# Landmark sums of two batches by adding DMA transfers, one path for the first batch's exponentials, more constants' products and a new order in a Nystrom attention and squared-ReLU kernel

## The chip, the core and the metric

The kernel runs on one core of a Trainium2 chip. The metric is the device time of one execution in microseconds (us). The profile of an execution gives the start and length of every instruction on the engines PE (TensorE's matmuls; PEld is its weight loads), DVE (VectorE), ACT (ScalarE), POOL (GpSimd) and SP (SyncE), and the DMA transfers.

## The reference: what is computed

q, k and v have 8 batches, 8 heads, 576 tokens and 64 columns. Per head, 32 landmarks are the means of 18 tokens each of q and of k. Three softmaxes follow: A (576 x 32, all queries against the key landmarks), B (32 x 32, landmarks against landmarks) and C (32 x 576, query landmarks against all keys). Z starts as B transposed over the product of two norms and goes through six steps of Z = 2 Z - Z B Z. The attention result A Z C v of all heads, 4608 tokens by 512 columns, goes through a block of two matrices.

```python
q_lm = q.reshape(B, H, m, S // m, D).mean(axis=3)     # m = 32, S // m = 18
k_lm = k.reshape(B, H, m, S // m, D).mean(axis=3)
A = sm(q, k_lm); Bm = sm(q_lm, k_lm); C = sm(q_lm, k)
for _ in range(6):
    Z = 2 * Z - Z @ Bm @ Z
x = A @ Z @ C @ v                                     # 4608 x 512 over all heads
g = np.maximum(x @ w_in, 0.0) ** 2                    # 4608 x 2048
out = g @ w_out
```

## The kernel before, in words

**One program, batch after batch.** All 8 heads of a batch lie on 128 partitions as 2 rows (r) of 4 heads (c) of 32 landmarks. POOL's queue issues all loads; most convert float32 to bf16 on the way. q and k of a batch go to X (`load_qk`, two transfers a tensor, L426), v to V (`load_v`, L442), the weights to w_in and w_out (L450, L457). There are three buffers of X and of V.

**The work of a batch** is a set of named operations, which carry the batch's number: T (transposes of q and k on DVE, L471), lm (landmark sums), lme (their scaling to bf16), lmt (their transpose), B, Bmx, Bsb, Bex, ... (softmax of B, L561 to L644), N and U (the six steps: N on PE at L713 or L718, U on DVE at L727; bd builds N's block-diagonal operand on POOL or DVE, L650), SC or SS (scores of C and A), Cmx, Cex, Cnr, CT (softmax of C), CV (C times v, L835), Zm and ZC (Z times that, L861, L869, L879, L882), W and We (times w_in, L906, and its copy out of PSUM to WP, L413, L417), SA, At, Amx, Asb, Aex, Asu, Arc, Aml, Ap, Ab (softmax of A and its transpose to AT). `ffn1` then multiplies WP with AT (F, L1079), takes the ReLU (R, L1100 on ACT or L1102 on DVE) and the square (Q, L1107 on ACT, L1109 on DVE or POOL) into G. `ffn2` multiplies G with w_out for 128 tokens at a time (O0 to O35 in four parts each, L1126), copies the sum (Oe) and stores it (St, SP's queue).

**Landmark sums.** Batches 0 to 2 add 18 tokens on PE with an identity (L502, L509). Batches 3 to 7 (`ROWS`) load q and k a second time: `load_xs` (L429) brings them as bf16 to XS, 96 partitions of 6 tokens for each head, in two transfers lx (L432), and `landmarks_rows` (L479) multiplies them with a 96 x 32 matrix of ones, 24 matmuls a batch (L487), into one bank of PSUM. One instruction then scales the sums to LM (lme, L415 on ACT or L419 on DVE).

**Softmax of A in batches 0 and 1.** It is computed with tokens on partitions, in two units u; batch 0 cuts each unit into a and b. The row maximum comes from `Amx` (L974) on DVE. Then either DVE subtracts it (Asb, L985) and ACT takes one exponential over all rows (Aex, L987), or, for the entries of `BY_ROW` (batch 0, unit 1, a and b), ACT takes the exponential row by row with the negative maximum as its bias, 10 instructions a piece (L980).

**The order is written out.** Every operation has a list of engines it may run on and costs in a small planner (`Plan`). The string `ORDER` gives the sequence of all operations, `/A`, `/D` or `/P` the engine where it isn't the first of its list, and `@` the PSUM bank. Each engine works off its share of that sequence in the planned order of starts and waits in place for whatever is late. POOL, too: a transfer that must wait for something holds up POOL's later loads and arithmetic. Software transfers use 8 slots in turn, and the ninth waits for the first to land.

**Constants' products.** Until the first O, the planner fills gaps of PE with matmuls of constants (`fillers`, `fill`, L1200), which write into a free bank and which nothing reads. A gap lies between the planned end of one operation and the planned start of the next, and products are added while the planned busy share of some stretch of 3.41 us is under a goal (0.55 before 30 us, 0.45 behind).

Of the kernel before, what the change touches and what calls it, by code (L numbers as in the profile page):

```python
# [264 lines left out]
def kernel(  # L265
# [195 lines left out]
    def attention(b):  # L461
# [477 lines left out]
        for u in range(2) if b in TOKENS else ():  # L939
# [27 lines left out]
            cuts = [0, 2 * n, 4 * n] if b in FIRST else [0, 4 * n]  # L967
            for j, (x0, x1) in enumerate(zip(cuts, cuts[1:])):
# [4 lines left out]
                op(f"Amx{b}.{u}{z}", {"DVE": v_(w)}, lambda e, s3=s3, p3_=p3_, pS=pS, at=at, neg=NM.get((b, u, z)):
                   nc.vector.tensor_reduce(s3(0)[:, at] if neg is None else neg[:, 0:at.stop - at.start],  # L974
                                           p3_(pS)[:, at], axis=AX.X, op=ALU.max, negate=neg is not None),
                   R=[pS], W=kx_("amx"))

                def rows(e, nm=NM.get((b, u, z)), sa3=sa3, p3_=p3_, pS=pS, x0=x0, x1=x1):
                    for x in range(x0, x1):
                        nc.scalar.activation(sa3[:, x], p3_(pS)[:, x], AF.Exp, bias=nm[:, x - x0:x - x0 + 1])  # L980
# [391 lines left out]
```

## Time and profile before

| what | us |
|---|---|
| median of 3 runs | 259.12 (259.1 to 259.36) |
| the profiled execution | 259.55 |
| its span in the profile | 257.8 |
| PE busy | 248.5 |
| DVE busy | 211.5 |
| ACT busy | 176.3 |
| POOL busy | 71.5 |
| loads on POOL's queue, MB | 24.25 |

The profiled execution's own time is 1.75 us above its span: that part lies around the instructions. Times of rows below are from the start of the span. A busy PE isn't PE at its peak, since the ends of matmuls are modelled. Consecutive instructions of one engine overlap by some tens of ns in the rows, so that the distance of two starts is the better measure of what one costs in a stream.

### The profile page before, as it was taken

What the parts mean: (1) busy time and instruction counts of PE and PEld (TensorE: products, weight loads), DVE (VectorE), ACT (ScalarE), POOL (GpSimd) and SP (SyncE); (2) the same over time, 40 slices, a digit from 0 to 9 for tenths busy, and PEclk for the clock granted to TensorE, in tenths of its full rate; (3) what the DMA queues carried; (4) which work ended last, traced back from release to release, by engine and by line L of the source; (5) the groups of instructions that cost most, each with busy time, mean ns of one, the idle gap of its engine ahead of it and who ended that gap; (6) DMA issues with size and microseconds to landing.
All of it is one profiled execution on the core that took longest, in us unless ns stands there. A gap on an engine that the chain in (4) does not pass through costs nothing.

```text
span 257.8 us, 7581 instructions
## 1 busy us (share of the span) xinstructions
PE 248.5 (96%) x3093; PEld 140.5 (54%) x3093; DVE 211.5 (82%) x549; ACT 176.3 (68%) x343; POOL 71.5 (28%) x122
## 2 busy tenths in 40 slices
PE   6979999999999999999999999999999999999993
PEld 2546565557554567465555466465454575466542
DVE  2779897987999999998998999888999989667221
ACT  3465779669896898888566499596663897357300
POOL 8566846643353260550210400021100100000000
PEclk9999999999999999999999999999999999999999
DMA  6999999999999999899613991025100350231044
GB/s 100 200 191 201 204 210 208 208 224 233 235 203 220 221 212 220 137 202 223 154 21 69 170 205 30 4 45 122 43 3 3 81 123 3 57 79 31 4 106 97
DMA packets 25123, 34.18 MB, mean 133 GB/s; under 512 B 2432, under 2 KB 14464, under 8 KB 25088
## 3 DMA queue, kind: packets, MB, share of 16 engines
q0 software_dynamic: 19168, 24.25, 55.6%
q1 hardware_dynamic: 5760, 9.31, 14.2%
q8 instruction: 24, 0.39, 0.6%
q10 hardware_dynamic: 160, 0.13, 0.2%
q14 instruction: 11, 0.09, 0.1%
HBM read 48.50 MB, written 9.44 MB: 225 GB/s over the span
## 4 chain that ended last, share of the span: by engine, by line
PE 84%; DVE 7%; DMA 3%; POOL 2%; issue 1%; ACT 1%; POOLq 0%
PE ps L1126 46%; PE ps L1079 23%; PE ps L906 3%; DMA X<-in_q_dram 3%; PE ps L835 2%; PE ps L487 1%; PE ps L749 1%; DVE SA L1032 1%; PE ps L713 1%; POOL X L426 1%; PE ps L1005 1%; PE ps L1200 1%; ACT SA L980 1%; PE ps L744 1%; PE ps L718 1%
## 5 line engine op out<-in xcount | busy, mean ns | idle before, releaser
L1126 PE MATMUL ps<-w_out,G 128*128 128x512 bf16 (+1 forms) x592 | 138.3, 374 | 0.0
L1126 PEld LDWEIGHTS <-G 128*128 128x128 bf16 x592 | 54.0, 98 | 54.7 <-issue 5.8
L1100 ACT ACTIVATE RS<-ps 128x576 bf16<-128x576 f32 (+2 forms) x104 | 63.7, 652 | 13.3 <-PE ps L1079 8.9
L1079 PE MATMUL ps<-AT,WP 128*128 128x288 bf16 (+2 forms) x512 | 72.0, 286 | 0.0
L1079 PEld LDWEIGHTS <-WP 128*128 128x128 bf16 x512 | 48.6, 98 | 20.6 <-issue 1.9
L1107 ACT ACTIVATE G<-RS 128x576 bf16<-128x576 bf16 (+2 forms) x54 | 35.9, 686 | 2.0 <-DVE RS L1102 1.6
L1109 DVE TENSOR_TENSOR G<-RS 128x576 bf16<-128x576 bf16 (+2 forms) x72 | 31.1, 447 | 6.8 <-ACT RS L1100 6.4
L471 DVE STREAM_TRANSPOSE TT<-X 128x576 uint32<-128x576 uint32 x32 | 24.0, 759 | 4.8 <-DMA X<-in_k_dram 4.2
L413 ACT CAST WP<-ps 128x1024 bf16<-128x1024 f32 (+1 forms) x23 | 21.8, 978 | 7.9 <-PE ps L906 7.8
L413 ACT COPY OS<-ps 128x512 f32<-128x512 f32 (+1 forms) x25 | 14.2, 571 | 18.1 <-PE ps L1126 18.0
L650 POOL TENSOR_TENSOR BD<-ST,blkb 128x256 bf16<-128x256 bf16 x15 | 10.9, 725 | 46.5 <-DVE ST L727 46.5
L790 ACT ACTIVATE C<-ps,sm 128x576 bf16<-128x576 f32 x16 | 14.4, 904 | 12.3 <-DVE sm L787 11.9
L1102 DVE TENSOR_SCALAR RS<-ps 128x576 bf16<-128x576 f32 (+2 forms) x24 | 17.9, 747 | 5.5 <-PE ps L1079 4.7
L442 POOL DMA_DIRECT2D V<-in_v_dram x24 | 12.9, 539 | 18.4 <-PE ps L835 15.1
L417 DVE COPY OS<-ps 128x512 f32<-128x512 f32 x12 | 8.3, 689 | 9.8 <-PE ps L1126 9.8
L727 DVE SCALAR_TENSOR_TENSOR ST<-ST,ps 128x128 bf16<-128x128 bf16 (+1 forms) x48 | 12.7, 264 | 2.6 <-PE ps L713 2.4
L1200 PE MATMUL ps<-onesb 128*128 128x512 bf16 (+1 forms) x38 | 11.9, 402 | 1.5 <-DVE onesb L349 1.5
L787 DVE TENSOR_REDUCE sm<-ps 128x1 f32<-128x576 f32 x16 | 11.8, 741 | 1.4 <-PE ps L718 1.2
L417 DVE CAST WP<-ps 128x1024 bf16<-128x1024 f32 (+1 forms) x11 | 12.2, 1119 | 0.3 <-PE ps L906 0.2
L1032 DVE STREAM_TRANSPOSE SA<-ps 128x320 f32<-128x320 f32 (+1 forms) x24 | 10.1, 456 | 0.3 <-PE ps L744 0.3
L906 PE MATMUL ps<-w_in,ZC 64*32 64x512 bf16 x256 | 10.2, 382 | 0.0
L426 POOL DMA_DIRECT2D X<-in_q_dram x16 | 8.9, 559 | 4.5 <-DVE sm L644 2.5
(144 smaller groups left out, 292.2 us busy)
## 6 DMA issues: line engine op xcount, KB each, us to landing
out_dram<-OS SPq DMA_DIRECT2D x70, 128.0 KB, 2.5
X<-in_k_dram POOLq DMA_DIRECT2D x16, 288.0 KB, 8.9
X<-in_q_dram POOLq DMA_DIRECT2D x16, 288.0 KB, 10.3
XS<-in_k_dram POOLq DMA_DIRECT2D x5, 576.0 KB, 9.6
XS<-in_q_dram POOLq DMA_DIRECT2D x5, 576.0 KB, 7.5
V<-in_v_dram POOLq DMA_DIRECT2D x8, 288.0 KB, 8.8
w_in<-in_moe_w_in_dram POOLq DMA_DIRECT2D x8, 256.0 KB, 10.3
w_out<-in_moe_w_out_dram POOLq DMA_DIRECT2D x4, 512.0 KB, 10.1
```

The lines of the kernel that those rows point to most:

```text
L413: nc.scalar.copy(o, i)
L417: eng(e).tensor_copy(o, i)
L471: op(f"T{b}.{t}{r}", {"DVE": v_(576) + 0.02}, lambda e, r=r: nc.vector.transpose(tt[:, t, r].rearrange("p s m e -> p (s m e)").bitcast(U32 ...
L790: op(f"Cex{b}.{r}", {"ACT": a_(576) + 0.27}, lambda e, r=r: nc.scalar.activation(Cs[r][:].rearrange("p x u -> p u x"), cbanks(r), AF.Exp, ...
L906: nc.tensor.matmul(ps[quad(pos_a(c, r)), pW.at + r, :], lhsT=zcs[r][half, pos_c(c, r), :], rhs=w_in[half, c, 512 * ch:512 * ch + 512], sta ...
L1079: nc.tensor.matmul(ps[:, ph.at + i, 0:w], lhsT=wp[:, r, 128 * ff:128 * ff + 128], rhs=at[:, r, t0:t0 + w], start=(r == 0), stop=(r == 1))
L1100: nc.scalar.activation(rs, pair(ph, w), AF.Relu)
L1102: nc.vector.tensor_scalar(out=rs, in0=pair(ph, w), scalar1=0.0, scalar2=None, op0=ALU.max)
L1107: nc.scalar.activation(g, rs, AF.Square)
L1109: eng(e).tensor_tensor(g, rs, rs, ALU.mult)
L1126: nc.tensor.matmul(bank(po)[:, 0:c1 - c0], lhsT=G[:, f, lo:lo + P], rhs=w_out[:, f, c0:c1], start=(f == 0), stop=(f == NF - 1))
L1200: nc.tensor.matmul(ps[:, j, 0:w], lhsT=onesb[:, 0:P], rhs=x[:, 0:w], start=True, stop=True)
```

## The change

**1. Adding transfers.** `ROWS` is cut to batches 3, 4, 5; batches 6 and 7 become `ADDED`. For them `load_sums` takes the place of `load_xs`: the 18 tokens of a landmark are three groups of 6, and three transfers a tensor, la6.00, la6.01, la6.02 (q) and la6.10, la6.11, la6.12 (k), bring one group each as float32 to the same place ACC. The first writes, the second and third add; each waits until the one before it has landed. ACC lies in the memory of XS (ACC of batch 6 in the half that held q, of batch 7 in the half that held k), so that the first also waits for the last reader of XS. DVE then adds 6 groups of 64 columns in two reduces a batch (lmc, 768 elements a partition) and lme scales them from SBUF. The 24 matmuls of each of the two batches are gone. The planner counts an adding transfer as 1.5 times 786432 bytes, which is what it counts for one lx.

**2. Exponentials of batch 0, unit 1.** `BY_ROW` is empty: 20 instructions of ACT go, two subtractions on DVE (Asb0.1a, Asb0.1b) and two exponentials over 320 elements on ACT come.

**3. Constants' products.** The goal before 30 us rises from 0.55 to 0.9. A gap begins where the planner's PE is free again, its wait for instructions included.

**4. The planner's fetch of PE's instructions** (256 in 6.2 us until 60 us, 3.8 until 110 us, 2.5 behind; before 6.2 until 140 us and 3.8 behind) **and a new order** of all operations, with other engines and banks: 8 more R on DVE, 6 fewer We, 4 fewer Cnr and 3 fewer Oe on DVE, 3 more Q of batch 0 on POOL among them.

```diff
-                    fetched = max(t, fetched + (self.FETCH_LOADED if t < LOADED else self.FETCH))
+                    fetched = max(t, fetched + (self.FETCH_LOADED if t < 60.0 else self.FETCH if t < 110.0 else 2.5))
...
-            a, b = o.start, o.start + o.engs["PE"]
+            a, b = o.start, o.end
...
-            if share(t) >= (0.55 if t < 30 else 0.45) or not near:
+            if share(t) >= (0.9 if t < 30 else 0.45) or not near:
...
-    XS = mk("XS", [96, 2, H, 6, D], BF16)
+    XS = mk("XS", [P, 2, H, 6, D], BF16)
+    ACC = [XS[:, i].rearrange("p h j d -> p (h j d)").bitcast(F32)
+           .rearrange("p (t r s d) -> p t r s d", t=2, r=2, d=D) for i in range(2)]
...
+    def load_sums(b):
+        for j in range(SEG // 6):
+            for t in range(2):
+                src = (q, k)[t][b].rearrange("(r c) (m s) d -> (c m) r (s d)", r=2, s=SEG)
+                op(f"la{b}.{t}{j}", {"POOL": 0.95}, lambda e, j=j, t=t, src=src: nc.gpsimd.dma_start(
+                    ACC[b % 2][:, t].rearrange("p r s d -> p r (s d)"), src[:, :, 6 * D * j:6 * D * (j + 1)],
+                    accum_op=ALU.add if j else ALU.bypass),
+                   R=[("ACC", b % 2, t)] if j else [], W=[("ACC", b % 2, t), *([] if j else [("XS", b % 2)])],
+                   nbytes=ADD_COST * 786432, queue="sw")
...
+        def landmarks_added():
+            acc, ls, kS = ACC[i2], LS[:, 0, 0:256].rearrange("p (t r d) -> p t r d", t=2, d=D), ("LS", 0)
+            for t in range(2):
+                op(f"lmc{b}.0{t}", {"DVE": v_(768)}, lambda e, t=t: nc.vector.tensor_reduce(
+                    ls[:, t], acc[:, t].rearrange("p r s d -> p r d s"), axis=AX.X, op=ALU.add),
+                   R=[("ACC", i2, t)], W=[(kS, t), (kS, "w")])
+            op(f"lme{b}.0", {"ACT": a_(256), "DVE": v_(256, True)}, lambda e: copy(e, lm[:], ls, scale=LMS),
+               R=[(kS, 0), (kS, 1)], W=[("LM", i2, r) for r in range(2)], port=("DVE",))
...
-ROWS = (3, 4, 5, 6, 7)
+ROWS = (3, 4, 5)
+ADDED = (6, 7)
+ADD_COST = 1.5
...
-BY_ROW = ((0, 1, "a"), (0, 1, "b"))
+BY_ROW = ()
...
```

The new order up to the first F's of batch 0 (from the maximum of B to F0.2), and the order before in the same stretch:

```
after:
Bcs0 Btr0 Cex0.0 Amx0.0b BBT0@7 Bnm0 SA0.1@1 Brn0 Yi0 Zi0/P Amx0.0a Asb0.0b win00 N0.0@4 Crc0 CT0.0 lm1.0@5
Aex0.0b win01 U0.0 Asb0.0a N0.1@6 Amx0.1a Aex0.0a lm1.0a win20 U0.1 Asb0.1a N0.2@7 Asu0.0a
Aex0.1a lm1.0b U0.2 T1.01 win21 N0.3@0 lme1.0 CV0@6,3 Cmk0 U0.3 Amx0.1b N0.4@5 Asu0.0b CVe0.0/A
lmt1.0 CVe0.1/A U0.4 bk1/P Arc0.0a Asb0.1b N0.5@5 B1@6 Arc0.0b CR0@4 Aex0.1b U0.5 Bmx1 Aml0.0b/P
CRe0/A Bsb1 Zd0@5 Asu0.1b Bex1 SA1.0@1 Zm0 Aml0.0a/P Bsu1 Asu0.1a ZC0@2 ldv2.11 Arc0.1b Amx1.0
Ap0.0@4 ZCe0 wout0 SA1.1@6 Arc0.1a Brc1 Ab0.0/A Aml0.1a Asb1.0 Bml1/P Aml0.1b/P Bmb1/A Aex1.0
W0.1@2 Amx1.1 W0.3@4 We0.1 Blo1/P ldv1.11 Ap0.1@0 Asb1.1 wout1 We0.3 F0.6@2 Ab0.1 ldk2.1 W0.0@6
R0.6 F0.4@4 wout2 We0.01/D We0.00 Bcs1@0 F0.20@2 R0.4 ldq2.1 Bnm1 Bad1 F0.2@6
before:
Bcs0 Btr0 Cex0.0 Amx0.1a BBT0@5
Bnm0 SA0.0@7 Brn0 Aex0.1a c8 Yi0 Zi0/P Amx0.1b win21 Amx0.0b N0.0@0 lm1.0@4 U0.0 Amx0.0a Asb0.0b
N0.1@1 Aex0.1b lm1.0a U0.1 win20 Asb0.0a CT0.0 N0.2@6 lm1.0b U0.2 T1.01 win31 N0.3@5 lme1.0 win30
U0.3 CV0@6,0 Aex0.0a Asu0.1a lmt1.0 Asu0.0a bk1/P CVe0.0/A B1@2 Asu0.1b N0.4@4 c10 Aex0.0b U0.4
Bmx1 Arc0.1a Bsb1 N0.5@5 Asu0.0b Aml0.1a/P Bex1 SA1.1@6 c14/A Bsu1 Arc0.1b Brc1 CVe0.1/A Crc0
U0.5 wout0 Cmk0 Aml0.1b CR0@2 Amx1.1 Zd0@4 Bml1/P CRe0/A Bmb1/A Zm0 Ap0.1@2 Blo1 Arc0.0a Arc0.0b
Asb1.1 Aml0.0a/P Bcs1@0 Ab0.1/A SA1.0@5 Btr1 Aml0.0b/P Aex1.1 Bnm1 Bad1 BBT1@3 Brn1 ldv1.11 ZC0@4
Yi1 Ap0.0@7 Zi1 ZCe0 Amx1.0 wout1 N1.0@6 Ab0.0/A W0.1@2 U1.0 W0.0@0 ldk2.1 Asb1.0 We0.1 N1.1@4
wout2 W0.2@6 U1.1 We0.01/D We0.00 ldk2.0 N1.2@5 F0.4@2
```

And three stretches of the new order around the adding transfers of batch 6:

```
la6.00 Q2.0 N3.4@1 F2.11@4 Aex3.0 R2.4/D O9.0@2 la7.00 lme5.0 U3.4 R2.11 bd3.5/D F2.8@6 Q2.4
...
F2.12@0 Q2.14/A Arc3.1 Arc3.0 ZC3@3 Aml3.0 O10.1
R2.12 la6.10 R2.15 ZCe3.0/D O10.2 Btr4 Ab3.0 ZCe3.1 Q2.15/A lmt5.0 la6.01 T4.01 W3.0@5 Q2.12/A
W3.3@3 W3.2@0 bt4/D ldq6.0 We3.0 O9.2 Aml3.1 ldq5.1 Bct4 Ab3.1 O9.3 We3.2 la7.10 T5.11 F3.2@5
We3.3 T4.00 O10.3 Bnm4 R3.2 Bad4 Brn4 BBT4@3 T5.10 F3.0@0 Zi4/P Oe9.0 ldk6.1 F3.1@4 Yi4 R3.0 St9
...
bd4.3/D R3.3 la6.02 Brc5 T4.10 O12.3 R3.5 Bml5/P F3.4@4 ldq7.1 Btf5 Oe12.0 Bcs5 F3.6@0 Q3.3
...
Q3.15/A bd5.2/D CV4@3,5 Asu4.1 N5.2@2 O14.3 Arc4.1 CVe4.1/A CVe4.0 T6.11 la6.12 ZC4@5 O13.3
Oe14.0 U5.2 ZCe4.0/D ldv6.10 bd5.3/D St14 ZCe4.1/D O15.3 Aml4.1 Oe13.0 ldk7.0 N5.3@2 ldv7.11
W4.0@3 Oe15.0 U5.3 W4.2@5 Ab4.1 ldq7.0 W4.3@0 We4.0 St15 Aml4.0 O16.0@2 la7.12 We4.2 O16.1 Ab4.0
St13 lmc6.00 bd5.4 We4.3 F4.0@3 W4.1@6 R4.0/D O16.2 We4.1 O16.3 lmc6.01 N5.4@3 SS5.0@0,4,6
lme6.0/D Oe16.0 U5.4 lmt6.0
```

More of the change, by code (lines that the diff above doesn't have):

```diff
@@ L1173, in loads @@
             load_xs(b)
+        elif what == "sums":
+            load_sums(b)
         elif what == "win":
@@ L1245 @@
-N0.1@1 Aex0.1b lm1.0a U0.1 win20 Asb0.0a CT0.0 N0.2@6 lm1.0b U0.2 T1.01 win31 N0.3@5 lme1.0 win30
-U0.3 CV0@6,0 Aex0.0a Asu0.1a lmt1.0 Asu0.0a bk1/P CVe0.0/A B1@2 Asu0.1b N0.4@4 c10 Aex0.0b U0.4
-Bmx1 Arc0.1a Bsb1 N0.5@5 Asu0.0b Aml0.1a/P Bex1 SA1.1@6 c14/A Bsu1 Arc0.1b Brc1 CVe0.1/A Crc0
-U0.5 wout0 Cmk0 Aml0.1b CR0@2 Amx1.1 Zd0@4 Bml1/P CRe0/A Bmb1/A Zm0 Ap0.1@2 Blo1 Arc0.0a Arc0.0b
-Asb1.1 Aml0.0a/P Bcs1@0 Ab0.1/A SA1.0@5 Btr1 Aml0.0b/P Aex1.1 Bnm1 Bad1 BBT1@3 Brn1 ldv1.11 ZC0@4
-Yi1 Ap0.0@7 Zi1 ZCe0 Amx1.0 wout1 N1.0@6 Ab0.0/A W0.1@2 U1.0 W0.0@0 ldk2.1 Asb1.0 We0.1 N1.1@4
```

210 lines of the change are left out of this document (106 added, 104 removed).

## The prediction

> **What bounds the kernel now.** I read the page first: the busy shares, the slices of PE and its clock, and the shares of the chain that ended last.
>
> ```profile
> PE 248.5 (96%) x3093; PEld 140.5 (54%) x3093; DVE 211.5 (82%) x549; ACT 176.3 (68%) x343; POOL 71.5 (28%) x122
> ...
> PE   6979999999999999999999999999999999999993
> ...
> PEclk9999999999999999999999999999999999999999
> ...
> PE 84%; DVE 7%; DMA 3%; POOL 2%; issue 1%; ACT 1%; POOLq 0%
> ```
>
> PE is busy from the second slice on at full granted clock, and the chain is PE for 84%. A gain must take work off PE or bring PE's own work forward. The table of windows says where that is possible.
>
> ```profile
> 18.00:24.00 6.00, 4.99 (x156) 3.46 (x158) 5.90 (x24) 4.11 (x19) 3.66 (x6) 1.00 1.19 185
> 24.00:30.00 6.00, 5.61 (x92) 3.19 (x92) 5.44 (x21) 3.35 (x8) 4.88 (x10) 1.00 1.24 206
> 36.00:42.00 6.00, 6.00 (x76) 3.78 (x75) 4.16 (x8) 4.40 (x8) 3.16 (x6) 1.00 1.17 210
> 102.00:108.00 6.00, 6.00 (x139) 2.87 (x128) 5.97 (x20) 4.20 (x9) 2.40 (x4) 1.00 0.79 127
> 132.00:138.00 6.00, 6.00 (x121) 2.81 (x120) 5.93 (x13) 3.25 (x8) 1.11 (x2) 1.00 0.53 85
> 252.00:258.00 6.00, 1.77 (x17) 1.35 (x14) 0.69 (x1) 0.37 (x1) 0.00 (x0) 0.94 0.38 83
> ```
>
> Columns: window, length, then busy time of PE, PEld, DVE, ACT and POOL, then clock, DMA share, GB/s. Before 30 us PE's business is partly constants, and DVE (5.90 of 6) is the engine that works without pause. From 36 us PE is full. The last window's PE ends about 4 us before the span does; that tail (copy, store, landing) keeps its form in the new order: the last four parts of O35, one copy, two stores.
>
> ```profile
> L1200 PE MATMUL ps<-onesb 128*128 128x512 bf16 (+1 forms) x38 | 11.9, 402 | 1.5 <-DVE onesb L349 1.5
> ```
>
> So the 30.5 us before the first F hold about 12 us of PE time that computes nothing. That start, the landmarks on PE, and a few waits in the middle are all that can be won.
>
> **Part 1, landmark sums: what goes.** The first and the last of five pieces of the chain show what a batch's 24 matmuls cost.
>
> ```profile
> 61.20 0.77 PE ps L487 x24
> ...
> 159.86 0.77 PE ps L487 x24
> ```
>
> Each is 0.77 us long, with PE's work directly before and behind. Batches 6 and 7 lose 2 x 0.77 = 1.5 us, at a place where PE is full: **-1.5 us**.
>
> **Part 1: what comes.** DVE gets two reduces of 768 elements a batch. The nearest rows:
>
> ```profile
> L1043 DVE TENSOR_REDUCE smA<-SA 128x20 f32<-128x640 f32 x6 | 4.8, 796 | 0.3 <-ACT SA L1041 0.3
> L1043 DVE TENSOR_REDUCE smA<-SA 128x16 f32<-128x512 f32 x6 | 4.0, 659 | 0.0
> ```
>
> From 512 to 640 elements a reduce grows by 137 ns, so 768 take some 0.93 us. Two a batch and two batches are 3.7 us of DVE; lme stays about what it was. DVE is nearly full there (5.93 and 5.97 of 6 us), but the new list also takes 6 We of 1.1 us and 3 Oe of 0.7 us off it and gives it 8 R of 0.75 us: its total hardly moves. PE need not wait as long as DVE's order holds, so I cost the reduces at 0; without that cover they cost up to 3.7 us.
>
> The transfers are the unknown. Nothing in this trace adds on the way. Nearest rows:
>
> ```profile
> XS<-in_k_dram POOLq DMA_DIRECT2D x5, 576.0 KB, 9.6
> XS<-in_q_dram POOLq DMA_DIRECT2D x5, 576.0 KB, 7.5
> ...
> DMA to landing us min/median/max: 6.4/9.3/14.7
> ```
>
> The third row is that of the line which issues XS. One adding transfer reads a third of the float32 bytes of an XS transfer and writes 384 KB instead of 576. If bytes alone count, it lands no later than XS does, 6.4 us; if reading back what is there costs as much again as an XS transfer, twice the median, 19 us. I take the median, 9.3 us: it lies in the stretch where the DMA share falls from 0.79 to 0.53, but three follow each other. Now the room. PE's work between two names of the new list is counted with rows of the chain: four O matmuls 0.86, F of batch 3 on 0.49, CV 0.76, a W (8 matmuls) 0.28.
>
> ```profile
> 102.25 0.76 PE ps L835 x72
> ...
> 110.33 0.56 PE ps L906 x16
> ...
> 118.05 0.49 PE ps L1079 x4
> 118.60 0.86 PE ps L1126 x4
> ```
>
> From la6.00 to la6.01 stand 5 O, 6 F, 1 CV: 8.0 us. From la6.01 to la6.02 6 O, 6 F, 4 W: 9.2 us. From la6.12 to the reduce that needs it (lmc6.01) 6 O, 1 F, 4 W: 6.8 us. At 9.3 us POOL waits 1.3 and 0.1 us at the two, which the next POOL work in the list (Zi4, some 4 us of PE later; Bml5, one O later) absorbs; DVE could wait 2.5 us at lmc6.01, but DMA has little queued there (0.53), so I go to the lower end for that one: below 6.8 us, no wait. Cost taken: **0**; bounds 0 and the price of the second rival.
>
> By the Trainium skill, "DMA: Bandwidth & Descriptors", section "Rules for kernel authors", an accumulating DMA reads its destination and writes it later with nothing holding the bytes in between, so each must wait for the semaphore of the one before; its section "Anatomy of one DMA" fits 2.0 us plus bytes over 436e3. By that fit 384 KB would land in an estimated 2.9 us, and no wait would be left; the row's 6.4 us as the minimum is longer.
>
> **Part 2, the exponentials, and the new order up to the first F.** The timeline of the stretch that sets the start:
>
> ```profile
> 14.76 0.66 POOL L450 DMA_DIRECT2D w_in<-in_moe_w_in_dram  x1
> ...
> 15.67 1.87 ACT L980 ACTIVATE SA<-ps,NM1a 128x32 f32<-128x32 f32 x10
> 16.01 0.23 DVE L674 TENSOR_TENSOR ST<-ps,sm 128x64 bf16<-128x64 f32 x1
> 17.57 0.49 DVE L974 TENSOR_REDUCE NM1b<-ps 128x10 f32<-128x320 f32 x1 [1.33 <-ACT SA L980]
> 17.98 0.41 DVE L974 TENSOR_REDUCE smA<-ps 128x8 f32<-128x256 f32 x1
> 18.31 0.28 DVE L727 SCALAR_TENSOR_TENSOR ST<-ST,ps 128x128 bf16<-128x128 bf16 x1
> 18.50 0.42 DVE L974 TENSOR_REDUCE smA<-ps 128x8 f32<-128x256 f32 x1
> ...
> 24.02 0.20 DVE L727 SCALAR_TENSOR_TENSOR ST<-ST,ps 128x64 bf16<-128x64 bf16 x1
> ```
>
> DVE sat idle 1.33 us until the row by row exponentials were done, and U0.0 (18.31) stood behind it. With one reader of that PSUM piece that wait goes, and two subtractions of 320 elements come. In a stream the starts lie 0.33 us apart for 256 elements (17.98, 18.31), 0.41 for 320 (17.57, 17.98), 0.19 for a U (18.31, 18.50). In the new list DVE has between Yi0 (16.01) and U0.5: five pieces of 256 (1.7), three of 320 (1.2), five U (0.95), CT 0.39, T 0.67, lmt 0.23, Cmk0 and three reciprocals (0.45): 5.6 us. With 0.2 for Yi0 and a little waiting U0.5 starts at 22.1 instead of 24.02, **1.9 us earlier**. Then Bmx1, Bsb1, one sum (0.7 us) and Zm0 at 23.0.
>
> ```profile
> 25.49 0.41 DVE L861 TENSOR_TENSOR ZM<-ps,CRS 128x256 bf16<-128x256 f32 x1
> 26.69 0.63 PE L955 MATMUL ps<-BK,TT 128*128 128x128 bf16 x8
> 27.16 0.70 PE L1200 MATMUL ps<-onesb 128*128 128x512 bf16 x3
> 27.79 0.22 PE L664 MATMUL ps<-Bt 32*32 32x32 bf16 x8
> 27.94 0.30 PE L879 MATMUL ps<-ZM,CV 128*64 128x32 bf16 x8
> 28.93 0.63 PE L906 MATMUL ps<-w_in,ZC 64*32 64x512 bf16 x16
> 29.41 2.42 ACT L413 CAST WP<-ps 128x1024 bf16<-128x1024 f32 x3
> 30.49 1.53 PE L1079 MATMUL ps<-AT,WP 128*128 128x256 bf16 x12
> ```
>
> ZM was ready at 25.9, yet ZC (27.94) stood on PE behind batch 1's scores and BBT1. The new list moves BBT1 and Bcs1 behind the first F. ZC0 then runs at 23.5, Ap0.0 and SA1.1 behind it (0.5 and 0.8), W0.1 at 25.2. What comes last is ACT's queue: Aex1.0 stands before We0.1 and needs Asb1.0, which DVE reaches 2.6 us after Zm0 (Asu0.1a 0.41, Amx1.0 and Asb1.0 0.6 each, Aml0.1a 0.5, small ones 0.5), at 25.9; Aex1.0 0.65, We0.1 1.0: F0.6 at **27.7 instead of 30.49, 2.8 us earlier**. The loads allow it, just: the pieces that W0.1 needs are now the second and fourth of w_in, the fourth is issued at 14.76, and the median to landing gives 25.1.
>
> ```profile
> w_in<-in_moe_w_in_dram POOLq DMA_DIRECT2D x8, 256.0 KB, 10.3
> ```
>
> Not all of that is kept. N1.0 to N1.2, Bcs1 and BBT1 (five rows of 0.2) and one more W (0.28) now run behind the first F: 1.2 us. And F0.2 waits for two copies to WP that start when W0.0 is done, about 0.4 us. Net **-1.2 us**. Bounds: 0 if DVE loses what the missing wait gave, -2.8 if the moved products fall into gaps.
>
> **Part 3, constants.** They fill gaps only; a product too many delays the next PE work by its length, 0.22 us for 512 columns at worst, and only where PE's next operand is ready earlier than planned. Cost taken 0, bounds 0 and +1 us. The granted clock is full without more of them, so nothing is gained either.
>
> **Part 4, the rest of the order.** One wait in the middle can go:
>
> ```profile
> 65.50 0.27 PE L744 MATMUL ps<-TT,LT 32*32 32x256 bf16 x1 [0.56 <-ACT RS L1100]
> ```
>
> The second half of batch 2's scores waited for ACT to free a bank. In the new list an O and more work stand between that F and SS2.0, and more again before SS2.1: -0.5 us. Loads come earlier for batches 3 and 4; the tightest, lx4.1 to lm4.0, keeps 10 O and 7 F, 12 us, against 9.6 us to landing. Unknown here: -1 to +4 us, since every engine waits in place.
>
> **Sum.** -1.5 - 1.2 - 0.5 = -3.2 us from the profiled execution's 259.55: 256.35. Its span is 257.8, 1.75 us lie around it and stay. The median shown is 0.43 us below the profiled run, so the time to compare is **255.9 us**.
>
> **Rivals.**
> - *The start gains nothing.* DVE is full from 18 to 30 us, and two subtractions join it. If Zm0 comes as late as before, only the landmarks and the bank wait remain, less the moved products: -1.5 - 0.5 + 1 = -1.0, **258.1 us**. Against it: 1.33 us of idle DVE and 2 us of ready ZM. Chance 0.20.
> - *The adding transfers become the wait (slower).* If each lands in 19 us, POOL stands 11 us at la6.01 and 10 us at la6.02, with X, V, Zi4 and Bml5 behind, and DVE, in order, 12 us at lmc6.01 with all R, Q and U behind it. PE can run on for perhaps 2 us. It decides from about 10 us at la6.12 (6.8 of room, 3.2 of gain to eat). At 14 us PE loses some 7 - 2 at lmc6.01 and 2 in POOL's part: +7, **263 us**. For it: three in a row were never run here; against it: a DMA share of 0.5. Chance 0.14.
> - *The new order waits elsewhere.* A late bank or operand in the middle, as the 0.56 us above but larger; 3 to 6 us eat the gain: **259 to 262 us**. Chance 0.16.
> - *More than said.* The moved products vanish in gaps and more bank waits go: -5, **254 us**. Chance 0.07.
>
> **How the numbers follow.** The forecast (254.5 to 257.5) has 0.43. Faster by over 0.2% (below 258.6), which is about what a measurement of this kernel can tell from no change: forecast 0.43, more 0.07, three quarters of the first rival, 0.15, together 0.65. Within 0.2%: 0.05 of it and 0.04 of the waiting order: 0.09. Slower: 0.14 and 0.12: 0.26. The range leaves out the upper part of the slow cases and the lower part of the best one: 253.9 to 261.5.
>
> **What would show it.** Right: L487 with 72 matmuls instead of 120; no L980; DVE without idle between 16 and 18 us; L879 near 23.5 and the first L1079 near 27.7 us; landings of the adding transfers under 9 us and no wait of DVE for them; PE full from 36 us. Wrong: POOL idle for a landing of its own adding transfer beyond 2 us, DVE waiting at the reduces, the first L1079 after 29.5, or windows after 36 us in which PE falls below 5.9.

## The result, and the profile after

| kernel | median, us | ratio to the kernel before, same chip | span of the profiled execution, us |
|---|---|---|---|
| before | 259.22 (259.1 to 259.36) | 1 | 257.8 |
| changed | 262.1 (261.81 to 263.53) | 1.0122 [1.0085, 1.0159] | 260.1 |

The change makes the kernel 1.2% slower, some 3.1 us, where 3.2 us faster were forecast: outside the range, and on the other side. From the page of the changed kernel, the busy shares, and the shares of the chain that ended last:

```profile
PE 249.1 (96%) x3051; PEld 139.4 (54%) x3051; DVE 217.0 (83%) x552; ACT 179.4 (69%) x326; POOL 82.7 (32%) x132
...
PE 72%; DVE 16%; DMA 4%; POOL 3%; issue 2%; ACT 2%; SPq 0%; DVEq 0%; POOLq 0%; ACTq 0%
```

PE has as much to do as before, but the chain is PE for 72% and no longer for 84%; DVE's part went from 7% to 16%. The windows of the changed kernel (columns as in the prediction) say where PE lacks work:

```profile
24.00:30.00 6.00, 5.05 (x73) 3.15 (x71) 5.56 (x14) 3.92 (x8) 5.76 (x10) 1.00 1.23 205
36.00:42.00 6.00, 5.28 (x40) 2.96 (x38) 6.00 (x7) 5.31 (x10) 3.25 (x4) 1.00 1.16 212
42.00:48.00 6.00, 4.98 (x72) 2.04 (x71) 5.25 (x15) 2.25 (x5) 5.48 (x7) 1.00 1.17 209
48.00:54.00 6.00, 5.67 (x159) 3.63 (x159) 4.42 (x18) 1.81 (x4) 3.38 (x5) 1.00 1.20 206
144.00:150.00 6.00, 5.44 (x87) 2.60 (x88) 5.97 (x14) 3.60 (x6) 1.81 (x2) 1.00 0.72 178
168.00:174.00 6.00, 5.55 (x49) 2.68 (x47) 5.86 (x14) 4.05 (x7) 1.76 (x3) 1.00 0.61 98
```

The kernel before had PE at 6.00 in each of the last five. So two places behind the first F lose: 36 to 54 us (2.1 us), and 144 to 174 us (1.0 us in these two windows). (The window 24.00:30.00, in front of it, comes back with few_constants below.) In the first place, DVE's 36.00:42.00 holds only 7 instructions in 6.00 busy us. The timeline of DVE there, then that of POOL:

```profile
36.12 0.77 DVE L483 STREAM_TRANSPOSE TT<-X 128x576 uint32<-128x576 uint32 x1
36.81 2.57 DVE L694 TENSOR_TENSOR ST<-Bf,sm 128x64 bf16<-128x64 f32 x1
39.30 0.76 DVE L483 STREAM_TRANSPOSE TT<-X 128x576 uint32<-128x576 uint32 x1
...
42.09 0.66 DVE L1015 TENSOR_REDUCE smA<-SA 128x16 f32<-128x512 f32 x1
42.68 0.86 DVE L377 TENSOR_TENSOR blk<-blkb 128x64 bf16<-128x64 bf16 x1
43.47 0.21 DVE L697 TENSOR_TENSOR ST<-ps,sm 128x64 bf16<-128x64 f32 x1
```

```profile
36.46 1.26 POOL L1135 TENSOR_TENSOR G<-RS 128x640 bf16<-128x640 bf16 x1
...
38.24 1.05 POOL L1135 TENSOR_TENSOR G<-RS 128x512 bf16<-128x512 bf16 x1
42.24 1.25 POOL L1135 TENSOR_TENSOR G<-RS 128x640 bf16<-128x640 bf16 x1 [2.96 <-DVE RS L1128]
```

L694 is Zi1, L377 is c8 (64 columns each), L1135 on POOL is a square Q of batch 0; the new order gives POOL five of them instead of two. Zi1 takes 2.57 us and ends with the second of two squares; c8 takes 0.86 us and ends with the third. Both read two tiles of SBUF. The transpose at 36.12 and the sum at 42.09, which run beside the same squares, read one tile of SBUF each and take what they take elsewhere (0.77 and 0.66 us). Who pays is seen in the waits of PE in the changed kernel (total us, times, longest):

```profile
PE ps L772 <- DVE RS L1128: 0.9, 1, 0.9
PE ps L741 <- DVE ST L697: 0.8, 1, 0.8
...
PE ps L736 <- DVE BD L673: 0.4, 1, 0.4
PE ps L858 <- issue: 0.3, 1, 0.3
```

The first two are the scores SC1.0 and the first step N1.0, at 42.2 and 43.7 us: late banks and late operands of a DVE that is 3 us behind. The third falls at 172.8 us and belongs to the second place, where the reduces of the landmark sums stand:

```profile
L509 DVE TENSOR_REDUCE LS<-XS x4: 1437/1460/1484, 142.9 to 169.8; 128x128 f32<-128x768 f32 x4
```

Minimum, median and maximum in ns: 1460, not the estimated 930. The adding transfers themselves were no trouble. Their line in the changed kernel shows the issues, who waited for them, and the landing:

```profile
L442 POOL DMA_DIRECT2D XS<-in_q_dram x6: 742/1228/1705, 99.9 to 147.6; - x6
L442 POOL DMA_DIRECT2D XS<-in_k_dram x6: 709/1261/1284, 105.6 to 138.9; - x6
...
  POOL XS L442: 0.7, 1
...
DMA to landing us min/median/max: 4.7/6.4/9.7
```

POOL waited 0.7 us, once, for its own earlier piece, and DVE never. (Before the first of them POOL also waited 4.6 us for the last reader of XS on PE.)

### The profile page after: what moved, and what is told of

Its sections match the earlier page's. It is cut to its first block, busy times and chain, and to the rows that moved or that the text cites. A ratio compares the mean times of both kernels' runs of the same rounds, so it can differ in the third digit from the quotient of the medians.

```text
span 260.1 us, 7502 instructions
## 1 busy us (share of the span) xinstructions
PE 249.1 (96%) x3051; PEld 139.4 (54%) x3051; DVE 217.0 (83%) x552; ACT 179.4 (69%) x326; POOL 82.7 (32%) x132
## 4 chain that ended last, share of the span: by engine, by line
PE 72%; DVE 16%; DMA 4%; POOL 3%; issue 2%; ACT 2%; SPq 0%; DVEq 0%; POOLq 0%; ACTq 0%
PE ps L1152 38%; PE ps L1105 21%; PE ps L929 3%; DMA X<-in_q_dram 3%; PE ps L858 2%; DVE sm L810 2%; DVE TT L483 1%; PE ps L772 1%; PE ps L1230 1%; DVE LS L509 1%; DMA out_dram<-OS 1%; PE ps L499 1%; POOL X L428 1%; PE ps L736 1%; DVE ZM L892 1%
## 5 line engine op out<-in xcount | busy, mean ns | idle before, releaser
L1126 ACT ACTIVATE RS<-ps 128x576 bf16<-128x576 f32 (+2 forms) x96 | 58.7, 652 | 14.6 <-PE ps L1105 10.5
L1133 ACT ACTIVATE G<-RS 128x576 bf16<-128x576 bf16 (+2 forms) x59 | 38.9, 682 | 3.1 <-DVE RS L1128 2.5
L415 ACT COPY OS<-ps 128x512 f32<-128x512 f32 (+1 forms) x28 | 16.2, 579 | 22.3 <-PE ps L1152 17.2
L1135 DVE TENSOR_TENSOR G<-RS 128x576 bf16<-128x576 bf16 (+2 forms) x64 | 27.9, 449 | 2.1 <-ACT RS L1126 1.3
L415 ACT CAST WP<-ps 128x1024 bf16<-128x1024 f32 (+1 forms) x29 | 26.8, 978 | 4.0 <-PE ps L929 3.7
L1128 DVE TENSOR_SCALAR RS<-ps 128x576 bf16<-128x576 f32 (+2 forms) x32 | 24.0, 752 | 3.6 <-PE ps L1105 1.7
L673 POOL TENSOR_TENSOR BD<-ST,blkb 128x256 bf16<-128x256 bf16 x12 | 8.4, 701 | 45.9 <-DVE ST L750 44.5
L419 DVE COPY OS<-ps 128x512 f32<-128x512 f32 (+1 forms) x9 | 5.7, 645 | 10.0 <-PE ps L1152 10.0
L736 PEld LDWEIGHTS <-BD 128*128 128x128 bf16 x72 | 6.4, 98 | 7.8 <-POOL BD L673 1.4
L428 POOL DMA_DIRECT2D X<-in_k_dram x16 | 9.7, 608 | 2.0 <-DVE BD L673 1.1
```

Source lines behind the costliest of these rows:

```text
L415: nc.scalar.copy(o, i)
L1126: nc.scalar.activation(rs, pair(ph, w), AF.Relu)
L1128: nc.vector.tensor_scalar(out=rs, in0=pair(ph, w), scalar1=0.0, scalar2=None, op0=ALU.max)
L1133: nc.scalar.activation(g, rs, AF.Square)
L1135: eng(e).tensor_tensor(g, rs, rs, ALU.mult)
```

## The experiments

The theory (A): what was lost is DVE standing still beside POOL's squares at 36 to 44 us, and reduces that are half as long again as thought on a DVE that has no room for them. Rivals: DVE simply has too much to do in the new order's start (B); the loss is all elsewhere (C), in the new order behind 47 us (D), or in the constants' products. All runs, each beside the kernel before on the same chip:

| run | edit | median, us | ratio | span, us |
|---|---|---|---|---|
| zi_apart | Zi1 on POOL, c8 early | 260.34 | 1.0022 [1.0007, 1.0038] | 258.7 |
| sq_on_dve | the five squares on DVE | 260.75 | 1.0042 [1.0023, 1.0061] | 258.8 |
| rows_67 | landmarks of 6, 7 on PE again | 262.05 | 1.0082 [1.0064, 1.01] | 260.1 |
| sum_straight | reduces without stride | 260.9 | 1.0052 [1.0029, 1.0075] | 259.0 |
| changed_again | none | 262.7 | 1.0109 [1.0068, 1.015] | 262.1 |
| fill_old | constants as before | 263.0 | 1.0132 [1.0091, 1.0174] | 260.9 |
| start_only | new order to 47 us, then the old | 260.24 | 1.002 [1.0, 1.0041] | 258.1 |
| zi_and_adds | zi_apart, adds for reduces | 259.07 | 0.9967 [0.9947, 0.9986] | 256.5 |
| added_alone | old order, adding transfers, adds | 262.09 | 1.01 [1.008, 1.0121] | 259.9 |
| zi_and_adds_again | as zi_and_adds | 258.99 | 0.9976 [0.9963, 0.9989] | 257.2 |
| few_constants | zi_and_adds, no constants after 8 us | 258.33 | 0.995 [0.9932, 0.9968] | 256.4 |
| fewer_late | zi_and_adds, none after 17 us | 259.78 | 1.001 [0.9995, 1.0025] | 257.6 |

**changed_again** gives the base. 

> The changed kernel once more, as the base beside which the runs on this chip are read: 1.012 of the kernel before, 262 us, with Zi1 near 2.6 us long on DVE and the gaps before SC1.0 and N1.0 near 1 us each. If the 1.012 came from few runs and not from the change, it comes out below 1.008.

It is 1.0109: the loss is the change's, about 1.1 to 1.2%. But the spans of the two profiled executions are 260.1 and 262.1 us, and the second shows why the times of this kernel scatter more than those of the kernel before. Windows of 1 us of changed_again:

```profile
25.00:26.00 1.00, 0.05 (x3) 0.04 (x4) 0.99 (x4) 0.00 (x0) 0.88 (x2) 0.99 1.25 205
26.00:27.00 1.00, 0.67 (x11) 0.66 (x12) 0.68 (x2) 0.27 (x1) 0.92 (x2) 0.50 1.24 210
...
28.00:29.00 1.00, 1.00 (x23) 0.34 (x20) 0.36 (x1) 0.68 (x3) 0.77 (x2) 0.50 1.22 206
```

PE does nearly nothing for a microsecond in front of ZC0 (0.05 of 1.00; ZC0 comes at 25.95), and then the granted clock is 0.50 for some 3 us, just where W and F come: the first F is at 30.19, not at 28.46. In the first profile the same stretch had a clock of 1.00. This isn't rare. Each execution's mean granted clock is on record: of the ten of the changed kernel (four of the first measurement, six of this one) four have 0.990 to 0.993 and take 263.3 to 263.9 us, and six have 0.997 to 1.000 and take 261.4 to 262.2 us. So a part of the loss in the medians is this, some 1.5 us in the executions that have it, and differences by ratios and by spans are both given below; the spans are compared with that of the first profile, whose clock was full at this place.

**zi_apart.** Only two small instructions move; the squares stay on POOL.

```diff
-Zi1 ... c8 SC1.0@4,6
+c8 SC0.1@4 ... Zi1/P ... SC1.0@4,6
```

> The changed kernel (262.1 us) with two small DVE instructions of batch 1's start taken away from POOL's squares of batch 0: Zi1 (2.57 us in the changed kernel's row, 0.21 usual) runs on POOL behind those squares, and c8 (0.86 us there, 0.17 usual) stands on DVE ahead of SC0.1. The five squares stay on POOL. Theory A (a DVE instruction that reads two tiles of SBUF stands still while POOL squares; PE loses 1.10 us before SC1.0 and 0.97 us before N1.0 by it): the two gaps shrink to under 0.5 us together, 260.1 to 260.7 us. Theory B (DVE simply has too much to do between 30 and 44 us in this order, the long row is only where it shows): DVE gets 0.2 us less, no more than 0.3 us faster, 261.8 to 262.1 us.

Measured: 1.0022, 0.9 to 1.0% (2.3 to 2.6 us) below the changed kernel; 1.4 us below its first profile by the spans, both at full clock. Part of the difference in the ratios is the clock, since only one of the twelve executions here has a mean below 0.996. From the timeline of POOL in this run:

```profile
36.71 1.27 POOL L1135 TENSOR_TENSOR G<-RS 128x640 bf16<-128x640 bf16 x1
37.93 0.29 POOL L694 TENSOR_TENSOR ST<-Bf,sm 128x64 bf16<-128x64 f32 x1
```

Zi1 runs as soon as POOL is free and takes 0.29 us. Its operands were there at 37.9 us at the latest in this run, while on DVE in the changed kernel it ended at 39.4: at least the last 1.4 us of the 2.57 were no wait for data. PE's waits before SC1.0 and N1.0 are gone. B, which had at most 0.3 us for this edit, is wrong.

**sq_on_dve.** The other side of the same question.

```diff
-Q0.0/P Q0.16/P Q0.18/P Q0.12/P Q0.30/P
+Q0.0 Q0.16 Q0.18 Q0.12 Q0.30
```

> The changed kernel with its five POOL squares of batch 0 (Q0.0, Q0.16, Q0.18, Q0.12, Q0.30) on DVE. Theory A (POOL's squares make DVE stand still for 2.36 + 0.69 us): DVE loses that standing and gets 5 squares of 0.42 to 0.49 us, 2.3 us: 0.8 us less work, Zi1 at 0.21 us, 261.0 to 261.8 us. Theory B (DVE has too much to do there): 2.3 us more on it, 263 to 264.5 us.

Measured: 1.0042, and 260.75 us, a little below the 261.0 to 261.8 of theory A. DVE does 2.3 us more and the kernel is faster; B had it slower. The timeline of DVE:

```profile
37.69 0.21 DVE L694 TENSOR_TENSOR ST<-Bf,sm 128x64 bf16<-128x64 f32 x1
...
41.93 0.18 DVE L377 TENSOR_TENSOR blk<-blkb 128x64 bf16<-128x64 bf16 x1
```

Same instructions, same engine, no squares on POOL: 0.21 for 2.57 and 0.18 for 0.86. By the Trainium skill, "SBUF — State Buffer", section "Who interferes with whom", a DVE instruction with two SBUF inputs fetches the second through ports that it shares with GpSimd, and whoever has them keeps them for the whole instruction. The rows agree, and go further in one point: Zi1 stood through two squares with 0.5 us between them, in which POOL issued a transfer.

**sum_straight.** The reduces read the same 768 elements in the order in which they lie, so they sum other ones: the landmarks of batches 6 and 7 are other numbers.

```diff
-ls[:, t], acc[:, t].rearrange("p r s d -> p r d s"), axis=AX.X, op=ALU.add)
+ls[:, t].rearrange("p r d -> p (r d)"),
+acc[:, t].rearrange("p r s d -> p (r s d)").rearrange("p (x s) -> p x s", s=6), axis=AX.X, op=ALU.add)
```

> The changed kernel with its four reduces of batches 6 and 7 reading six neighbours in memory instead of six elements 256 bytes apart (they sum other elements, so the landmarks of these two batches are other numbers; same counts and sizes). If the stride makes them 1.46 us instead of the estimated 0.93, each falls to 0.9 to 1.0 us and PE gets some 0.5 to 1.0 us of the gaps at 146 to 148 and 171.9 us back: 261.1 to 261.6 us. If the operand's place or type makes it, they stay at 1.46 us and the time at 262.1 us. If DVE's reduces cost PE nothing, they fall and the time stays.

Measured: 1.0052 (260.9 us, a little below the range expected), and the line of the reduces:

```profile
L509 DVE TENSOR_REDUCE LS<-XS x4: 908/926/942, 143.0 to 168.8; 128x128 f32<-128x768 f32 x4
```

926 ns: the prediction's 0.93 was right for elements that lie together, and the 256 bytes from one element to the next cost 0.53 us a reduce, 2.1 us of DVE in all. PE got 1.1 us of span (0.6 to 0.7% in the ratios) back; the wait of 0.4 us at 172.8 is gone. The same page of the Trainium skill (section "Door 1: The DMA port swizzle") says that each access which crosses into a new 16-byte line of SBUF pays a penalty; the row agrees, without showing which size of step begins to pay.

**rows_67.**

```diff
-ROWS = (3, 4, 5)
-ADDED = (6, 7)
+ROWS = (3, 4, 5, 6, 7)
+ADDED = ()
```

(lx at the places of la6.00, la6.10 and la7.02, one of them a little later; the matmuls where the first reduce stood, in banks 5 and 1.) 

> The changed kernel with the landmark sums of batches 6 and 7 on TensorE again, as in the kernel before (XS transfers, 24 matmuls a batch), all else in the new order. Theory A (four reduces of 1.46 us on a full DVE cost PE about as much as the matmuls did): PE gets 2 x 0.77 us back, the gaps between 146 and 148 us (1.2 us) and at 171.9 us (0.6 us) go: between 0.5 us faster and 0.2 us slower than the changed kernel, 261.6 to 262.3 us. Theory C (the landmarks' 1.5 us were gained, the loss is all elsewhere): 263.4 to 263.9 us.

Measured: 1.0082, 0.3 to 0.4% below the changed kernel with intervals that overlap, and the same span. The 2 x 0.77 us of matmuls are back (pieces of the chain of rows_67),

```profile
142.70 0.77 PE ps L499 x24
...
166.50 0.77 PE ps L499 x24
```

and the kernel is no slower for it: the strided reduces took from PE at least what the matmuls had taken. C, which had it 1.5 us slower, falls.

**fill_old.**

```diff
-a, b = o.start, o.end
+a, b = o.start, o.start + o.engs["PE"]
...
-if share(t) >= (0.9 if t < 30 else 0.45) or not near:
+if share(t) >= (0.55 if t < 30 else 0.45) or not near:
```

> The changed kernel with the constants' products counted as in the kernel before (goal 0.55 and the planned length, not 0.9 and the planned end). If the constants cost nothing, the first F stays at 28.4 to 28.6 us and the time at 262.1 us within 0.3. If the products too many delay PE work near the start (the six more at 0.22 us), the first F comes 0.5 to 1.2 us earlier and the time is 261 to 261.6 us.

Measured: 1.0132 against 1.0109, with intervals that overlap almost wholly; the median, 263.0 us, lies above the 262.1 within 0.3 that was expected, and the first F comes at 29.3 us, not at 28.4 to 28.6. The rule for the constants makes no difference in the time that these runs show. In this order it doesn't even take products away: the old rule places two more than the new one (51 for 49). (The page of fill_old lists fewer matmuls of PE, 3011, but 3053 weight loads, two more than the changed kernel's 3051; some matmul records are missing from this trace.)

**zi_and_adds.** Zi1 and c8 as in zi_apart, and per batch three additions instead of two reduces.

```diff
-nc.vector.tensor_reduce(ls[:, t], acc[:, t].rearrange("p r s d -> p r d s"), axis=AX.X, op=ALU.add)   # t = 0, 1
+nc.vector.tensor_tensor(av[:, :, 0:3], av[:, :, 0:3], av[:, :, 3:6], ALU.add)
+nc.vector.tensor_tensor(l4, av[:, :, 0], av[:, :, 1], ALU.add)
+nc.vector.tensor_tensor(l4, l4, av[:, :, 2], ALU.add)
```

> The changed kernel with Zi1 on POOL and c8 early, as in the run before, and with the four reduces of 1.46 us replaced by adds of pieces that lie together: per batch one tensor_tensor of 768 elements and two of 256, some 1.2 + 2 x 0.35 = 1.9 us for 2.9. Theory A (POOL's squares and the stride of the reduces are the loss): zi_apart's gain of 1.4 us in the span and 1.0 us more, 259.4 to 259.9 us, level with the kernel before. Theory D (the order after 47 us loses the rest): above 260.5 us.

Measured: 0.9967 (259.07 us, a little better than the 259.4 to 259.9 of theory A), and 0.9976 the second time. 

> The kernel of zi_and_adds once more, beside added_alone on the same chip: 0.995 to 0.999 of the kernel before, and below added_alone by 0.5 us or more only if the new order and start are worth something by themselves.

The three additions take 934, 580 and 426 ns, 1.94 us a batch for 2.92. The two repairs add up: 0.9 to 1.0% for the one and some 0.5% more for the other, against a loss of 1.1 to 1.2%, and with both the changed kernel is 0.2 to 0.3% faster than the kernel before. D falls: the new order behind 47 us is all in this kernel.

**start_only.** ORDER is the new one up to B2 (with Zi1 and c8 as in zi_apart) and the old one for all that is left; Zd1 takes bank 7 for 3. The landmarks are on PE. 

> The new order up to B2 (some 47 us), with Zi1 on POOL and c8 early, and from there the order of the kernel before with its landmarks on TensorE. Theory A (the start is worth what the prediction said, 2.0 us less 0.8 to 1.2 us of products moved behind the first F, and the loss is POOL's squares and the reduces): 0.8 to 1.2 us faster than the kernel before, 258.0 to 258.5 us. Rival (an earlier first F is given back in batch 1 in any case, since DVE has its own work to do there): 259.0 to 259.5 us. Theory D (the new order after 47 us is what loses most): also 258 to 258.5 us, and the next kernel of this call, which keeps that order, stays above 260.5 us.

Measured: 1.002, so the start brings nothing here; 260.24 us is above the range of theory A and above that of its rival. The first F comes at 28.50 (before: 30.49), but the first W of batch 1 at 56.4 (before: 56.2). What lies between, by the groups of PE's work from the first F to that W, first of the kernel before (30.49:56.22),

```profile
L718 PE MATMUL ps<-ST 32*32 32x64 bf16 (+1 forms) x24 | 0.7, 186 | 0.0
```

then of start_only (28.50:56.4):

```profile
L741 PE MATMUL ps<-ST 32*32 32x64 bf16 (+1 forms) x48 | 1.4, 191 | 0.0
...
L687 PE MATMUL ps<-Bt 32*32 32x32 bf16 x8 | 0.2, 178 | 0.0
...
L653 PE MATMUL ps<-Blo,blkb 128*128 128x64 bf16 x1 | 0.2, 194 | 0.0
L653 PE MATMUL ps<-Bb,blkb 128*128 128x64 bf16 x1 | 0.2, 193 | 0.0
```

N1's three steps are 0.7 us, BBT1 and Bcs1 0.4 to 0.6, the moved W 0.28: about 1.5 us, for which the prediction had 1.2. Then 0.3 us for WP (it had 0.4), and one more wait, at CV1:

```profile
51.85 0.25 PE L858 MATMUL ps<-V,CT 32*64 32x128 bf16 x3
52.60 0.80 PE L858 MATMUL ps<-V,CT 32*64 32x128 bf16 x69 [0.51 <-DVE ZM L884]
```

The profile names DVE's ZM, but CV1 neither reads ZM nor writes the bank that ZM is computed from; the cause isn't shown, and the splice of two orders may have made it. Without this wait the start would have been worth some 0.2 to 0.5 us. So this run shows that most of the 2.0 us go back to the moved products, and leaves open whether those few tenths remain.

**added_alone.** The old order with the landmarks of batches 6 and 7 by adding transfers and the three additions, the transfers spread over 104 to 149 us. 

> The kernel before, in its own order, with only the landmark sums of batches 6 and 7 brought by adding transfers and summed by the adds of zi_and_adds (0.93 + 0.58 + 0.43 us a batch); the transfers stand at new places in POOL's queue, found for this order, and the sums where the matmuls stood. If the landmarks alone are worth their 2 x 0.77 us of PE: 257.6 to 258.3 us, 0.994 to 0.997 of the kernel before, like zi_and_adds, and the new order is then worth nothing by itself. If DVE's 3.9 us or POOL's 12 issues of 1.2 us hold PE up in this order: 259 to 261 us. If the adding transfers land late, DVE shows idle time for DMA at the first add.

Measured: 1.01, and 262.09 us: above what the first case had, and above the second's 259 to 261 us too (1.01 of 259.2 is 261.8). A window of this run, and the wait of PE in it:

```profile
162.00:168.00 6.00, 4.67 (x43) 1.91 (x41) 5.54 (x16) 3.09 (x8) 0.00 (x0) 1.00 0.01 3
```

```profile
163.55 0.39 PE L1158 MATMUL ps<-w_out,G 128*128 128x512 bf16 x1 [1.08 <-DVE G L1141]
```

PE stands 1.08 us for a square that DVE has late, right behind the additions of batch 7 (161.3 to 163.1 us). No DVE instruction waits for an adding transfer; POOL waited 5.2 us for its own earlier pieces. So at this one placement in the old order, taking the landmarks off PE costs more than it brings; other places for the transfers and sums weren't tried. What it is worth in the new order is seen only beside POOL's squares: sum_straight (landmarks off PE, reduces of 0.93 us) has 1.0052 and rows_67 (landmarks on PE) 1.0082 on the same chip, 0.3%, with intervals that just overlap. No run has the new order with Zi1 and c8 moved and the landmarks on PE.

**few_constants.** zi_and_adds shows one more wait, of PE at CV1, for nothing that the trace names (the "issue" at L858 in the changed kernel):

```profile
50.45 0.79 PE L867 MATMUL ps<-V,CT 32*64 32x128 bf16 x64
51.72 0.26 PE L867 MATMUL ps<-V,CT 32*64 32x128 bf16 x8 [0.48 <-issue]
```

```diff
-            if not n:
+            if not n or at > 8.0:
```

> The kernel of zi_and_adds without the constants' products behind 8 us: 27 matmuls and as many weight loads fewer in PE's list, so that every block of 256 instructions ends 27 matmuls later in the work. In that kernel PE stands 0.67 us inside CV1, behind its 64th matmul, waiting for nothing that the trace shows, some 2.2 to 2.5 us after a 16 KB packet of the instruction queue began. Theory E (it waits for its next block of instructions): that gap leaves CV1, and is under 0.2 us or stands later among O or Ap. Theory F (it is an operand of CV1 that is late): it stays inside CV1 at 0.5 to 0.7 us. And the products themselves: if they cost nothing and bring nothing, the granted clock stays at 1.00 between 8 and 30 us, the first F comes at 27.5 to 28.2 us, and the time is 0.993 to 0.998 of the kernel before; if they hold the clock up, it falls below 1.00 behind 10 us and the time rises by 1 us or more.

Measured: 0.995, the fastest kernel of the study. CV1 in this run:

```profile
50.96 0.83 PE L867 MATMUL ps<-V,CT 32*64 32x128 bf16 x72
```

All 72 go through. By itself this doesn't exclude a late operand (F), since CV1 also begins 0.5 us later here. The place of the wait in the other kernels decides it. In the eight runs with the whole new order and 49 products, CV1 begins anywhere from 50.45 to 54.60 us, and PE stops behind the 64th of its 72 matmuls every time, when 734 weight loads (PEld) have been done. In fill_old, with two products more ahead, it stops behind the 62nd, again with 734 loads done. In few_constants the 734th load comes after CV1, and no pause of this kind is seen there. A wait that keeps its place in PE's list while the work moves by 4 us is one for PE's own instructions, as theory E says.

There is an earlier one of the same kind, which the kernels all have: near 25 us the weight loads stop behind the 351st in each of the fourteen runs, the kernel before included, whatever operation stands there. The row of PEld with which each goes on, of before, after, changed_again, few_constants and fewer_late in turn:

```profile
26.61 0.11 PEld L630 LDWEIGHTS <-blkb 128*128 128x128 bf16 x2 [0.72 <-issue]
25.20 0.20 PEld L902 LDWEIGHTS <-CV 128*64 128x64 bf16 x7 [0.64 <-issue]
25.95 0.29 PEld L902 LDWEIGHTS <-CV 128*64 128x64 bf16 x7 [1.50 <-issue]
26.87 0.13 PEld L938 LDWEIGHTS <-ZC 64*32 64x32 bf16 x13 [0.53 <-issue]
25.97 0.74 PEld L987 LDWEIGHTS <-TT 128*128 128x128 bf16 x7 [1.46 <-issue]
```

In the new order the place falls on ZC0 (L902), which the first F needs: ZM was ready at 24.36, the first weight load of ZC0 was done at 24.57, and the matmuls begin at 25.20, behind a pause of PE of 0.67 us that the profile puts down to a sum on DVE. In fewer_late, with 13 products fewer, ZC0 goes through at 23.62, and the pause comes at the next scores instead.

The clock, though, is not free. Windows of few_constants:

```profile
12.00:18.00 6.00, 4.48 (x77) 3.22 (x78) 5.45 (x20) 2.83 (x9) 4.06 (x8) 0.89 1.11 206
18.00:24.00 6.00, 5.16 (x152) 3.38 (x151) 4.86 (x19) 2.54 (x8) 2.89 (x5) 0.83 1.17 190
24.00:30.00 6.00, 5.14 (x72) 3.14 (x70) 5.55 (x14) 4.08 (x8) 5.98 (x12) 1.00 1.23 204
```

The granted clock (the third column from the end) is 0.89 and 0.83, where zi_and_adds had 1.00, and the first F comes at 28.50 instead of 27.99. The two effects nearly cancel; the gain over zi_and_adds is 0.2%, which these runs don't tell from nothing, since the intervals overlap.

**fewer_late** tried to have both: no products behind 17 us (`at > 17.0`). 

> The kernel of zi_and_adds without the constants' products behind 17 us only: 13 fewer, so that the end of the block of instructions falls among the O matmuls behind CV1 and the products that held the clock between 12 and 17 us stay. Theory E (a block of instructions is late at CV1): no gap above 0.2 us in CV1, and with the clock at 0.95 to 1.00 between 12 and 24 us the first F comes at 27.5 to 28.1 us: 0.992 to 0.995 of the kernel before, 0.3 us or more better than both few_constants and zi_and_adds. If the clock falls as far as in few_constants (0.83 between 18 and 24 us), it is level with that kernel, 0.995.

Measured: 1.001. CV1's wait is gone here too, but the window

```profile
24.00:30.00 6.00, 4.70 (x51) 2.46 (x51) 4.42 (x10) 3.72 (x7) 5.63 (x10) 0.72 1.24 206
```

shows a granted clock of 0.72 around the first F (28.93), as changed_again did with all products in place. Behind the pause at the 351st weight load the clock is 0.50 for some 3 us here as there. The two have the longest pauses of PE at this place, 1.27 us here and 1.53 us in changed_again; behind those of 0.60 to 1.07 us, in the nine other profiles in which ZC0 meets it, the clock stayed at 1.00. So in these profiles the clock fell with the long pause, which isn't shown to be its cause by an edit. It happens oftener here: eleven of the twelve executions have a mean granted clock of 0.982 to 0.985, and the profiled one has 0.993; the median is 0.4% above zi_and_adds. The expectation held only in its part on CV1.

## Why the prediction was wrong, step by step

- **"Each is 0.77 us long ... -1.5 us"**: right. L499 has 72 matmuls less 48, and rows_67 shows the same 0.77 us coming back twice.
- **"768 take some 0.93 us ... I cost the reduces at 0"**: this step failed, in size and in cover. The nearest rows had their elements together, the reduce of the change has them 256 bytes apart; they took 1.46 us, 5.8 us for four. The bound for lost cover was 3.7 us. "PE need not wait as long as DVE's order holds" held for 0.93 us a piece, as sum_straight shows, more than for 1.46: 0.6 to 0.7% of the loss (1.1 us in the spans).
- **The squares that the new order gives to POOL had no term at all.** They are a part of "the rest of the order", which the prediction costed at -0.5 us with "-1 to +4 us, since every engine waits in place". It asked what a moved step does to its own queue, not what it does to an engine that reads the same memory at the same time. This is the largest failure: 0.7 to 1.0% in the ratios (1.7 to 2.6 us, with some of the clock in it), 1.3 to 1.4 us in the spans.
- **The first F**: 28.46 instead of 27.7, 2.0 us earlier instead of 2.8, and only 0.3 us earlier (30.19) in an execution in which the clock fell. ZC0 ran at 25.20, not at 23.5, for two reasons: ZM, its operand, was computed at 23.95 where the prediction had 23.0, and PE then stood 0.67 us for its own instructions, for which the prediction had no term. "Net -1.2 us": the products behind the first F took back about 1.5 us, the copies to WP 0.3, and a wait at CV1 0.35 (in the changed kernel) to 0.67, so that nothing is left. The first rival ("the start gains nothing") had this part right, for a different reason: the F came earlier, and it didn't help.
- **The adding transfers**: right, with 0.7 us of waiting on POOL where 1.3 and 0.1 were worked out, and a median landing of 6.4 us (4.7 to 9.7) where 9.3 was taken. The slower rival was wrong: no run shows DVE or PE waiting for one of them.
- **"Constants ... Cost taken 0"**: no difference between the two rules is shown (fill_old), with two things overlooked: the products count in PE's list of instructions, and so decide which operation meets the waits behind the 351st and the 734th weight load; and "the granted clock is full without more of them" was read off the old order, where the first of these pauses was 0.39 us of PE, while in the new one it is 0.6 to 1.5 us, and the clock fell in four of ten executions.
- **"-0.5 us" for the bank wait at 65.50**: that wait is gone, as forecast; waits of 0.3 to 0.5 us in front of N steps (for BD) came in its place.
- **The rivals.** "The new order waits elsewhere ... 259 to 262 us", with late banks and operands in the middle, describes what happened, and 262.1 us lies at its end; 0.16 was too little for it. DVE was at 5.9 of 6 us in three of the quoted windows, which left no room for what came late.

Signs for "wrong" that the prediction named came true: windows behind 36 us with PE below 5.9. Of the signs for "right", L499, the absence of the row by row exponentials and most of the landings (the longest took 9.7 us, not under 9) are there; ZC0 near 23.5 and the first F near 27.7 us are not.

What stays open: the squares cost 1.3 to 2.6 us and the reduces 1.1 to 1.8 us, by spans or by ratios, and how much of the difference is the clock around 26 us isn't settled. Why the pause in front of ZC0 is 0.67 us in one execution of the changed kernel and 1.53 us in another isn't known. That POOL's issue of a transfer between two squares keeps DVE standing is seen once and wasn't tried.

## What to carry to other kernels

Work moved to an idle engine isn't free: look at what runs beside it and reads the same memory, above all on an engine that the rest waits for, and take a row of 2.57 us for 64 columns as a sign of it. Price a reduce from a row with the same step between its elements, and on an engine that is full in the window take its whole length as a cost, not nothing. When work is brought forward, list what moves behind it, and follow the lead to a later mark in the same work (here the first W of the next batch) before counting it. A pause that stays behind the same count of instructions from kernel to kernel, while the operation behind it changes, belongs to the list of instructions and not to an operand.

## What the hardware showed that I hadn't expected

- A DVE instruction with two operands in SBUF stood still beside POOL's squares: 2.57 us for 0.21, 0.86 us for 0.18.
- A reduce of 768 float32 elements takes 1.46 us with 256 bytes from element to element, 0.93 us with none.
- Adding transfers of 384 KB land in 4.7 to 9.7 us (median 6.4), no later than plain loads of this kernel; each takes POOL 0.7 to 1.7 us to issue, where a plain load takes about 0.6 to 0.8.
- PE stood for its own instructions behind the 351st weight load in all fourteen runs (its weight loads paused for 0.4 to 1.5 us) and behind the 734th in the nine with the new order's CV1 there (0.35 to 0.67 us); 27 or 13 matmuls fewer ahead moved the first to another operation and left CV1 without a wait.
- The granted clock was 0.50 for some 3 us behind a pause of PE of 1.53 us in one execution of the changed kernel, and 1.00 behind one of 0.67 us in another; without the products behind 8 us it was 0.89 and 0.83 between 12 and 24 us. Where it falls decides what it costs.
